# Second batch's attention: scores of pairs 2 to 4 in one piece each, ahead of the preceding pair's weighted sums, with a fourth buffer for exponentials

## The chip, the cores and the metric

The kernel runs on one core of one Trainium2 chip. The metric is the device time of one execution in microseconds (us); the kernel before took 550.68 us, the median of three runs. Five engines work side by side: TensorE (PE in the profile; PEld is its weight loading), VectorE (DVE), ScalarE (ACT), GpSimd (POOL) and SyncE, whose queue (SP) issues all DMA transfers of this kernel. Each executes its own instructions in order and waits on semaphores for the others.

## The reference

Attention for 4 batches x 8 heads, 768 positions, 64 features a head. A query sees the keys less than 16 positions away and, for each of 24 blocks of 32 positions, one block key (the elementwise maximum of the block) with one block value (the mean). The result, with the heads side by side (768 x 512 a batch), goes through a mixer of tokens and then of channels:

```python
k_sum = k.reshape(B, H, nb, block, D).max(axis=3)
v_sum = v.reshape(B, H, nb, block, D).mean(axis=3)
scores_all = np.concatenate([scores_l_m, scores_s], axis=-1)   # local (masked), blocks + log(block)
a = np.exp(scores_all - max); a = a / (sum(a) + 1e-09)
x = np.matmul(a, v_all)
h = np.maximum(xt @ w_tok1, 0.0) @ w_tok2
u = x + h.transpose(0, 2, 1)
h2 = np.maximum(u @ w_ch1, 0.0) @ w_ch2
return u + h2
```

All is float32; the kernel gets that accuracy on TensorE by splitting operands into a high and a low part and adding three products.

## The kernel before

**Attention.** Heads go in pairs: pair p holds heads n = 2p and 2p + 1, and batch b holds pairs 4b to 4b + 3. So batch 1, the "second batch" of the title, holds pairs 4 to 7. A pair's 12 query tiles of 64 rows are taken in two halves g of six. A query tile meets 96 local keys and 24 block keys, 120 columns. `scores` (L439) writes 24 matmuls a half, or 48 in one piece for both (tiles `sc_n_g`, one PSUM bank each); DVE subtracts and finds the lowest (`lowest`), ACT takes the exponentials (`power`) into the buffer `e_p_g`, with a sum in `den`. The exponentials are then turned: in batch 1 by TensorE (`turn_halves`, L521: `et_*` in PSUM, `eT_*` in SBUF), in batches 2 and 3 by DVE and a way through HBM (`turn_blocks`, L581: a transpose on DVE, a store `away_*`, and four fetches `eT_*`). `weighted` (L618) multiplies with the values (`av_n`, L637). `turn_x` and `fetch_x` send the result through HBM to have it turned: `xaway_b_half_p`, and back as `xT_b_half_p` in four fetches, issued in L608.

**Mixer.** `tok1x` (L818) makes token products: for each g three groups `t1q_b_g` of 12 matmuls on operand sets xs and ws, which ACT and POOL split, in a ring "u0" with four places (two sets). `split_t1` makes the two parts of `t1` from it (L784 on ACT, L789 on DVE). `tok2` (L872) multiplies with w_tok2 (`up_b_half_p`, L895); DVE adds it to `xT` (L912), ACT and DVE split the sum into `u`. Channel mixing runs over two halves of the tokens (512 and 256) and 12 blocks f of 128 channels: `ch1` (L947, `hp_b_half_f`, L956), a rectifying split into `h` on ACT and DVE, `ch2` (L983, `acc_b_half_o`, L999). At the end of a half DVE and POOL add `u` (L1030, L1038), and the result goes out (L1049).

**What sets the order.** Every operation is recorded by `add` with an estimated duration, what it reads and writes, and a rank; `Plan._order` schedules the list by these estimates, and every engine's instructions, the DMA issues on SP too, are written in that order and executed in it. The program records 24 slots of channel mixing for each batch (2 halves x 12 blocks f) and, at given slots, steps of the next batch's attention (`att_step`, L700: "s" scores, "e" turning, "a" weighted sums), token products (t1s), and up pieces (u1s, t2s). For batch 1 the steps follow `ORDER`, in halves, spread over the slots by a count (want); for batches 2 and 3 `PLACES` gives slots. Buffers are rings: "e" has 3 places for e, eT and xT; "h" 2; "u0" 4. PSUM banks rotate too: in the second half of a batch's slots the scores, the turnings, t1q and up share four banks (`att_bank`, `tok_bank`).

Of the kernel before, what the change touches and what calls it, by code (L numbers as in the profile page):

```python
# [15 lines left out]
AF = mybir.ActivationFunctionType  # L16
# [4 lines left out]
B, H, S, D = 4, 8, 768, 64  # L21
# [55 lines left out]
class Plan:  # L77
# [48 lines left out]
    def _order(self):  # L126
# [19 lines left out]
        while events:  # L146
# [5 lines left out]
            for e, queue in queues.items():  # L152
# [50 lines left out]
def tile_attention_mixer(  # L203
# [22 lines left out]
    def sbuf(shape, tag, name, bufs, dtype=F32):  # L226
        return plan.slot(sb, shape, dtype, tag, name, bufs)
# [211 lines left out]
    def scores(p, gs, behind=()):  # L439
# [3 lines left out]
        for g in gs:  # L443
            e = e_t[p, g] = sbuf([P, 2, HS], "e", f"e_{p}_{g}", 3)
# [243 lines left out]
    ORDER = [("s", 0, 0), ("s", 0, 1)]  # L688
    for hp in range(NP):
        more = hp + 1 < NP  # L690
        ORDER += [("e", hp, 0)] + [("s", hp + 1, 0)] * more
        ORDER += [("e", hp, 1), ("a", hp, 0)] + [("s", hp + 1, 1)] * more
    PAIR = [("s", None), ("e", 0), ("e", 1), ("a", 0)]
    STEPS = len(ORDER)
    FIRST = list(ORDER)
    for hp in range(NP - 1):
        at = FIRST.index(("a", hp, 0))
        FIRST[at : at + 2] = FIRST[at + 1], FIRST[at]

    def att_step(b, s, behind=()):  # L700

        if b >= FAR:
            hp, (kind, g) = s // 4, PAIR[s % 4]
        else:
            kind, hp, g = (ORDER if b else FIRST)[s]
# [936 lines left out]
    PLACES = {2: {}, 3: {}}  # L1642
    for b, ss, aa in ((2, (-1, 2, 6, 11), (0, 6, 11, 17)), (3, (-1, 2, 6, 11), (2, 6, 11, 14))):
        for hp in range(NP):
            PLACES[b].setdefault(ss[hp], []).extend(range(4 * hp, 4 * hp + 3))
            PLACES[b].setdefault(aa[hp], []).append(4 * hp + 3)
    start = [sum(HT[0][j // NF] // 256 for j in range(i)) for i in range(2 * NF + 1)]
    for b in range(B - 1):
        done = 0
# [16 lines left out]
        for slot, (half, f) in enumerate(seq):  # L1666
# [59 lines left out]
            if b == B - 3 and slot >= 2 * NF - 5:  # L1726
                weight_away(slot - 2 * NF + 5)
            if b == B - 2 and slot >= NF + 5:
                weight_away(slot - NF)
            if b == B - 2 and slot == 22:  # L1730
                last_sums()
            if slot == 2 * NF - 1 and b + 2 < B:
                for s in PLACES[b + 2].get(-1, ()):
                    att_step(b + 2, s, here)
# [64 lines left out]
```

## Time and profile before

| | us |
|---|---|
| runs of the kernel before | 550.59, 550.68, 554.17; median 550.68 |
| the profiled execution, its own time | 552.68 |
| its span in the profile | 550.2 |
| PE busy | 536.8 (98%) |
| DVE, POOL, ACT busy | 341.9, 268.1, 267.9 |

The profile shows one execution. Its span begins with the first and ends with the last instruction that the profiler recorded; the execution's own time is 2.5 us longer. A stretch of the span can be looked at alone, for busy time and for TensorE's granted clock. The chain of waits follows the work that ended last back through what released each step; its pieces have the length from their start to the start of the next piece, so a group of matmuls is a little shorter there than in the timeline, where matmuls are pipelined and ends are modelled.

### The profile page before, as it was taken

What the parts mean: (1) busy time and instruction counts of PE and PEld (TensorE: products, weight loads), DVE (VectorE), ACT (ScalarE), POOL (GpSimd) and SP (SyncE); (2) the same over time, 40 slices, a digit from 0 to 9 for tenths busy, and PEclk for the clock granted to TensorE, in tenths of its full rate; (3) what the DMA queues carried; (4) which work ended last, traced back from release to release, by engine and by line L of the source; (5) the groups of instructions that cost most, each with busy time, mean ns of one, the idle gap of its engine ahead of it and who ended that gap; (6) DMA issues with size and microseconds to landing.
All of it is one profiled execution on the core that took longest, in us unless ns stands there. A gap on an engine that the chain in (4) does not pass through costs nothing.

```text
span 550.2 us, 12919 instructions
## 1 busy us (share of the span) xinstructions
PE 536.8 (98%) x4649; PEld 479.6 (87%) x4649; DVE 341.9 (62%) x954; ACT 267.9 (49%) x771; POOL 268.1 (49%) x348
## 2 busy tenths in 40 slices
PE   7999999999999999989999999999999999999997
PEld 4789888878999987868899997888899999999997
DVE  4996779666656664535473363635264387687886
ACT  4897888755664331404062341414153354666652
POOL 2656688713037020488696321169888512445111
PEclk9999999999999999989999999999999999999999
DMA  8953788654657385867777756655858553643521
GB/s 324 397 201 116 220 270 238 222 171 146 210 178 222 63 239 106 231 172 233 214 261 184 189 194 152 207 120 174 198 160 219 149 222 125 195 141 118 189 97 57
DMA packets 148127, 103.46 MB, mean 188 GB/s; under 512 B 101216, under 2 KB 126048, under 8 KB 148064
## 3 DMA queue, kind: packets, MB, share of 16 engines
q1 hardware_dynamic: 147920, 102.55, 62.7%
q8 instruction: 36, 0.59, 0.4%
q14 instruction: 27, 0.22, 0.1%
q10 hardware_dynamic: 144, 0.10, 0.1%
HBM read 70.96 MB, written 29.88 MB: 183 GB/s over the span
## 4 chain that ended last, share of the span: by engine, by line
PE 85%; DMA 5%; DVE 5%; SPq 1%; POOL 1%; issue 1%; ACT 0%; DVEq 0%; ACTq 0%; POOLq 0%
PE hp L956 25%; PE acc L999 25%; PE up L895 5%; PE t1q L851 5%; PE av L637 4%; PE pb L1234 3%; PE qb L1234 3%; PE sc L468 3%; PE qc L1234 2%; PE pa L1234 2%; PE pc L1234 2%; PE qa L1234 2%; PE t1p L803 2%; DMA k<-in_kw 2%; DMA vw<-in_vw 2%; DVE t L1078 1%
## 5 line engine op out<-in xcount | busy, mean ns | idle before, releaser
L999 PE MATMUL acc<-h,w 128*128 128x512 f32 (+1 forms) x864 | 161.7, 336 | 0.7 <-DVE h L973 0.7
L956 PE MATMUL hp<-u,w 128*128 128x512 f32 (+1 forms) x864 | 160.8, 337 | 0.3 <-DVE h L973 0.3
L999 PEld LDWEIGHTS acc<-h,w 128*128 128x128 f32 x864 | 132.6, 188 | 19.4 <-issue 1.4
L956 PEld LDWEIGHTS hp<-u,w 128*128 128x128 f32 x864 | 133.5, 189 | 18.3 <-issue 0.8
L968 ACT ACTIVATE h<-hp 128x512 fp32r<-128x512 f32 (+1 forms) x72 | 35.3, 490 | 128.2 <-PE hp L956 120.0
L492 ACT ACTIVATE e<-e,den 128x120 f32<-128x120 f32 x192 | 69.9, 384 | 45.8 <-DVE den L482 43.7
L973 DVE SCALAR_TENSOR_TENSOR h<-hp,h 128x512 fp32r<-128x512 f32 (+1 forms) x72 | 39.9, 554 | 75.8 <-ACT h L968 75.4
L1076 POOL TENSOR_TENSOR s<-s,w 128x256 f32<-128x256 f32 x84 | 61.6, 739 | 5.2
L482 DVE CUSTOM_DVE_ANT_0 e<-sc,mask_sb 128x120 f32<-128x120 f32 x192 | 41.2, 277 | 14.4 <-PE sc L468 14.1
L1038 POOL TENSOR_TENSOR ot<-ot,u 128x512 f32<-128x512 f32 (+1 forms) x24 | 23.7, 1013 | 37.1 <-DVE ot L1030 16.4
L837 POOL TENSOR_TENSOR xs<-x,xs 128x512 fp32r<-128x512 f32 x18 | 23.3, 1294 | 35.1 <-ACT xs L832 35.0
L1605 POOL TENSOR_TENSOR w<-wb,w 128x256 fp32r<-128x256 f32 x48 | 34.5, 740 | 10.9 <-ACT w L1599 10.6
L895 PE MATMUL up<-wt,t 128*128 128x512 f32 (+2 forms) x192 | 38.0, 340 | 0.9 <-DVE den L482 0.9
L895 PEld LDWEIGHTS up<-wt,t 128*128 128x128 f32 x192 | 30.8, 189 | 3.8 <-PE sc L468 1.1
L420 DVE TENSOR_REDUCE vs<-vb 96x8 f32<-96x256 f32 (+1 forms) x40 | 18.2, 458 | 22.0 <-DMA vb<-in_vb 21.7
L637 PEld LDWEIGHTS av<-v,eT 120*64 120x64 f32 x768 | 24.7, 141 | 6.1 <-issue 5.0
L637 PE MATMUL av<-v,eT 120*64 120x64 f32 (+1 forms) x768 | 27.3, 228 | 2.2 <-DMA eT<-away 2.1
L851 PE MATMUL t1q<-xs,ws 128*128 128x256 f32 x216 | 28.5, 282 | 0.0
L492 ACT ACTIVATION_READ_ACCUMULATOR e<-e,den 128x1 f32 x144 | 27.2, 189 | 0.0
L851 PEld LDWEIGHTS t1q<-xs,ws 128*128 128x128 f32 x216 | 26.9, 190 | 0.1
L837 POOL TENSOR_TENSOR ws<-wt,ws 128x512 fp32r<-128x512 f32 x18 | 23.7, 1319 | 4.1 <-ACT ws L832 4.0
L468 PE MATMUL sc<-k,q 64*64 64x120 f32 x768 | 24.8, 268 | 0.9 <-DVE k L1078 0.8
(131 smaller groups left out, 833.5 us busy)
## 6 DMA issues: line engine op xcount, KB each, us to landing
w<-in_w_ch SPq DMA_DIRECT2D x48, 256.0 KB
k<-in_kw SPq DMA_DIRECT2D x16, 720.0 KB
v<-in_vw SPq DMA_DIRECT2D x24, 288.0 KB
q<-in_q SPq DMA_DIRECT2D x16, 384.0 KB
away<-e SPq DMA_DIRECT2D x16, 384.0 KB
eT<-away SPq DMA_DIRECT2D x64, 96.0 KB
sums<-s SPq DMA_DIRECT2D x24, 256.0 KB
w2d<-w SPq DMA_DIRECT2D x12, 512.0 KB
```

The source lines that it names most:

```text
L468: nc.tensor.matmul(tiles[g, j].t[c * QT : (c + 1) * QT, i * NC : (i + 1) * NC], lhsT=qt.t[rows, t * QT : (t + 1) * QT], rhs=kt.t[rows, t, ...
L482: nc.vector.tensor_tensor_reduce(out=e_t[p, g].t[:, j, i * P : i * P + NC], in0=tiles[g, j].t[:, i * NC : (i + 1) * NC], in1=mask_sb[:, mv ...
L492: nc.scalar.activation(ei, ei, AF.Exp, bias=den_t[n].t[:, 1, T : T + 1], scale=-1.0, accum_out=den_t[n].t[:, 0, T : T + 1] if p >= NP else ...
L637: nc.tensor.matmul(pv[cs, T], lhsT=eT(T % (TT // 2), c), rhs=v.t[:NC, 2 * T + c], start=True, stop=True,)
L837: lambda slot=slot, src=src: nc.gpsimd.tensor_tensor(out=slot.t[:, 1], in0=src(), in1=slot.t[:, 0].bitcast(F32), op=ALU.subtract),
L851: nc.tensor.matmul(pt.t[:, 2 * P * k : 2 * P * (k + 1)], lhsT=ws[:, wp, T, ks], rhs=xs[:, xp, T], start=(c == 0 and k == 0 and T == 0 and ...
L895: nc.tensor.matmul(pt.t[:, :nt], lhsT=t1.t[:, part, ks], rhs=wt2[w].t[:, k, h0 : h0 + nt], start=(far and k == 0 and i == 0), stop=(k == D ...
L956: nc.tensor.matmul(pt.t[:, :nt], lhsT=w1_t[f].t[:, w, c], rhs=us[c].t[:, part], start=(i == 0), stop=(i == len(ops) - 1),)
L973: lambda: nc.vector.scalar_tensor_tensor(out=h.t[:, 1], in0=pt.t[:, :nt], scalar=0.0, in1=h.t[:, 0].bitcast(F32), op0=ALU.max, op1=ALU.sub ...
L999: nc.tensor.matmul(slot.t[:, c0 : c0 + nt], lhsT=w2_t[f].t[:, w, o * P : (o + 1) * P], rhs=h.t[:, part], start=(f == 0 and w == 0 and part ...
L1076: nc.gpsimd.tensor_tensor(out=out_, in0=left, in1=right, op=op)
L1234: nc.tensor.matmul(bank_.t[:, cs], lhsT=w(i), rhs=x(j)[:, cs], start=first and n == 0, stop=True, skip_group_check=True,)
```

## The change

Scores of pairs 5 to 7 (2 to 4 of batch 1) are recorded as one piece of 48 matmuls instead of two of 24, ahead of the weighted sums of the preceding pair (`LAPPED`); since both halves of a pair's exponentials are then alive beside the turned ones of the preceding pair, the second half of each takes its place in the ring "h" instead of "e". The turnings of pairs 5 and 6 are one job on TensorE (both halves); those of pairs 4 and 7 stay in halves. The slots of batch 1's steps stand in a table, and slots of the steps around them move: weighted sums of batches 2 and 3, the token products of batch 1 (t1s of b = 0), up pieces of second halves (u1s), values loads of batch 3 and weight stores by a slot. The planner counts 0.4 us more for a DMA whose issue takes over 0.6 us. Batch 0's own steps keep their order under another notation (`FIRST`).

```diff
-                    w.end = dma + self.LAND
+                    w.end = dma + self.LAND + (0.4 if w.took > 0.6 else 0.0)
...
-            e = e_t[p, g] = sbuf([P, 2, HS], "e", f"e_{p}_{g}", 3)
+            tag, bufs = ("h", 2) if g and NP < p < 2 * NP else ("e", 3)
+            e = e_t[p, g] = sbuf([P, 2, HS], tag, f"e_{p}_{g}", bufs)
...
-    def turn_halves(p, g):
+    def turn_halves(p, gs):
...
         add(
-            "pe", 0.7, flip, reads=[(e, part) for part in PARTS],
-            writes=[(pt, 0) for pt in banks], rank=R_H,
+            "pe", 0.35 + 0.35 * len(gs), flip,
+            reads=[(e, part) for e, _, _ in parts for part in PARTS],
+            writes=[(pt, 0) for _, _, banks in parts for pt in banks], rank=R_H,
         )
...
+    HALVED = (0, 3)
+    PAIR = [("s", None), ("e", None), ("a", 0)]
+    def att_step(b, step, behind=(), halves=False):
...
+        elif kind == "e" and b < FAR:
+            for gs in [(0,), (1,)] if halves or hp in HALVED else [(0, 1)]:
+                turn_halves(p, gs)
...
+    LAPPED = [("s", 0, 0), ("s", 0, 1), ("e", 0, None)]
+    for hp in range(1, NP):
+        LAPPED += [("s", hp, None), ("a", hp - 1, 0), ("e", hp, None)]
+    LAPPED += [("a", NP - 1, 0)]
+    for step, at in zip(LAPPED, (9, 10, 11, 12, 13, 13, 13, 15, 15, 17, 17, 17, 18)):
+        PLACES[1][at].append(step)
+    for b, ss, aa in ((2, (-1, 2, 6, 11), (2, 6, 11, 19)), (3, (-1, 2, 6, 11), (2, 6, 9, 14))):
...
-            a0, a1 = 20, 30
-            t1s = (20, 22)
+            t1s = (17, 23)
...
-            u1s = ((2, 2, 3, 3), (0, 1, 2, 4))[b - 1]
+            u1s = ((1, 2, 3, 3), (0, 2, 3, 5))[b - 1]
...
-            if b == 1 and 1 < slot <= 17:
-                vb_step(3, slot - 2, here)
-            if b == 1 and 1 <= slot < 17:
-                vb_load(3, slot - 1)
+            if b == 1 and 2 < slot <= 18:
+                vb_step(3, slot - 3, here)
+            if b == 1 and 2 <= slot < 18:
+                vb_load(3, slot - 2)
...
-            if b == B - 3 and slot >= 2 * NF - 5:
-                weight_away(slot - 2 * NF + 5)
-            if b == B - 2 and slot >= NF + 5:
+            if b == B - 3 and slot >= 2 * NF - 4:
+                weight_away(slot - 2 * NF + 4)
+            if b == B - 2 and slot >= NF + 4:
```

What this does to the order on the engines is shown at three places. Lines of the changed kernel have numbers 2 higher; the last number in a name only tells buffers apart.

**1. TensorE, batch 1's attention, from the scores of pair 6 (`sc_12`, `sc_13`) on.** Of each group the first row is given. Before:

```order
L468 MATMUL sc_12_0_2099<-k_6_1775,q_6_1780 64x120
...
L956 MATMUL hp_0_1_3_2113<-u_0_1_0_1007,w1_3_1193 128x256 x3
...
L999 MATMUL acc_0_1_0_1994<-h_0_1_2_2064,w2_2_1145 128x256 x6
...
L637 MATMUL av_10_2158<-v_10_1954,eT_5_0_2084 64x64 x6
...
L468 MATMUL sc_12_1_2192<-k_6_1775,q_6_1780 64x120
...
L956 MATMUL hp_0_1_4_2211<-u_0_1_0_1007,w1_4_1236 128x256 x3
...
L535 MATMUL et_6_0_0_2231<-identf_66,e_6_0_2126 120x64
...
L999 MATMUL acc_0_1_0_1994<-h_0_1_3_2154,w2_3_1206 128x256 x6
...
L468 MATMUL sc_14_0_2274<-k_7_2018,q_7_2036 64x120
...
L956 MATMUL hp_0_1_5_2290<-u_0_1_0_1007,w1_5_1302 128x256 x3
...
L535 MATMUL et_6_1_0_2315<-identf_66,e_6_1_2225 120x64
```

After:

```order
L469 MATMUL sc_12_0_2180<-k_6_1775,q_6_1780 64x120
...
L469 MATMUL sc_12_1_2182<-k_6_1775,q_6_1780 64x120
...
L1001 MATMUL acc_0_1_0_1908<-h_0_1_4_2163,w2_4_1263 128x256 x6
...
L958 MATMUL hp_0_1_6_2237<-u_0_1_0_1007,w1_6_1371 128x256 x3
...
L641 MATMUL av_10_2261<-v_10_2048,eT_5_0_2143 64x64 x6
...
L1001 MATMUL acc_0_1_0_1908<-h_0_1_5_2208,w2_5_1318 128x256 x6
...
L958 MATMUL hp_0_1_7_2321<-u_0_1_0_1007,w1_7_1416 128x256 x3
...
L539 MATMUL et_6_0_0_2344<-identf_66,e_6_0_2226 120x64
...
L539 MATMUL et_6_1_0_2346<-identf_66,e_6_1_2251 120x64
...
L1001 MATMUL acc_0_1_0_1908<-h_0_1_6_2278,w2_6_1403 128x256 x6
...
L958 MATMUL hp_0_1_8_2395<-u_0_1_0_1007,w1_8_1481 128x256 x3
...
L469 MATMUL sc_14_0_2413<-k_7_1977,q_7_1983 64x120
```

The second half of the scores moved up to the first (24 + 24 matmuls, one piece), ahead of pair 5's weighted sums (`av_10`), and the two turnings `et_6_0` and `et_6_1` stand together. Each step stands three to four blocks f of batch 0's channel mixing later than before.

**2. TensorE and SP, the turn from batch 0 to batch 1.** On TensorE from the last token products (`t1q_1_1`) to the first channel mixing of batch 1 (`hp_1_0_0`), of each group the first row (of the scores the first and the last tile's). Before:

```order
L851 MATMUL t1q_1_1_2717<-xs_1_1_1_2713,ws_1_1_1_2731 128x256 x12
L851 MATMUL t1q_1_1_2717<-xs_1_1_2_2746,ws_1_1_2_2749 128x256 x12
L956 MATMUL hp_0_1_10_2796<-u_0_1_0_1007,w1_10_1605 128x256 x3
...
L999 MATMUL acc_0_1_0_1994<-h_0_1_9_2686,w2_9_1588 128x256 x6
...
L895 MATMUL up_1_0_2_2842<-wt2_0_810,t1_1_2_2812 128x512
...
L895 MATMUL up_1_0_3_2851<-wt2_0_810,t1_1_3_2814 128x512
...
L956 MATMUL hp_0_1_11_2861<-u_0_1_0_1007,w1_11_1662 128x256 x3
...
L999 MATMUL acc_0_1_0_1994<-h_0_1_10_2834,w2_10_1637 128x256 x6
...
L468 MATMUL sc_16_0_2899<-k_8_2528,q_8_2534 64x120
...
L468 MATMUL sc_17_1_2902<-k_8_2528,q_8_2534 64x120
...
L999 MATMUL acc_0_1_0_1994<-h_0_1_11_2893,w2_11_1692 128x256 x6
...
L956 MATMUL hp_1_0_0_2960<-u_1_0_0_2791,w1_0_929 128x512 x3
```

After:

```order
L1001 MATMUL acc_0_1_2_1909<-h_0_1_11_2677,w2_11_1692 128x256 x6
L853 MATMUL t1q_1_1_2808<-xs_1_1_0_2762,ws_1_1_0_2778 128x256 x12
L897 MATMUL up_1_0_0_2828<-wt2_0_810,t1_1_0_2796 128x512
...
L897 MATMUL up_1_0_1_2844<-wt2_0_810,t1_1_1_2798 128x512
...
L853 MATMUL t1q_1_1_2808<-xs_1_1_1_2803,ws_1_1_1_2821 128x256 x12
L853 MATMUL t1q_1_1_2808<-xs_1_1_2_2838,ws_1_1_2_2842 128x256 x12
L897 MATMUL up_1_0_2_2912<-wt2_0_810,t1_1_2_2901 128x512
...
L897 MATMUL up_1_0_3_2923<-wt2_0_810,t1_1_3_2905 128x512
...
L469 MATMUL sc_16_0_2941<-k_8_2408,q_8_2411 64x120
...
L469 MATMUL sc_17_1_2944<-k_8_2408,q_8_2411 64x120
...
L958 MATMUL hp_1_0_0_2972<-u_1_0_0_2891,w1_0_929 128x512 x3
...
L958 MATMUL hp_1_0_1_3009<-u_1_0_0_2891,w1_1_1030 128x512 x3
```

The last five groups of batch 0's channel mixing (hp 10 and 11, acc 9 to 11) stood among these pieces; they now stand ahead of them all, the last of them directly ahead of `t1q_1_1`. On SP, the fetches of `xT_1_0_*` and the writes of batch 0's second output half (`out_0<-ot_0_1_0`), before:

```order
L608 DMA xT_1_0_2_2752<-xaway_1_0_2_2466 32x16x32 x4
L291 DMA vb_2_11_2793<-in_vb 96x256
L608 DMA xT_1_0_3_2810<-xaway_1_0_3_2688 32x16x32 x4
L291 DMA vb_2_12_2849<-in_vb 96x256
L291 DMA vb_2_13_2876<-in_vb 96x256
L608 DMA xT_1_1_0_2927<-xaway_1_1_0_2013 32x8x32 x2
L291 DMA vb_2_14_2937<-in_vb 96x256
L291 DMA k_10_2941<-in_kw 128x1440
...
L1049 DMA out_0<-ot_0_1_0_2957 128x256
L608 DMA xT_1_1_1_2987<-xaway_1_1_1_2246 32x8x32
L1049 DMA out_0<-ot_0_1_0_2957 128x256 x2
```

After:

```order
L612 DMA xT_1_0_2_2785<-xaway_1_0_2_2595 32x16x32 x2
L291 DMA vb_2_13_2801<-in_vb 96x256
L612 DMA xT_1_0_2_2785<-xaway_1_0_2_2595 32x16x32 x2
L1051 DMA out_0<-ot_0_1_0_2780 128x256
L612 DMA xT_1_1_0_2835<-xaway_1_1_0_2092 32x8x32 x2
L291 DMA vb_2_14_2852<-in_vb 96x256
...
L612 DMA xT_1_1_1_2871<-xaway_1_1_1_2342 32x8x32 x2
L291 DMA vb_2_15_2888<-in_vb 96x256
L1051 DMA out_0<-ot_0_1_0_2780 128x256
L612 DMA xT_1_1_1_2871<-xaway_1_1_1_2342 32x8x32
L1051 DMA out_0<-ot_0_1_0_2780 128x256
L612 DMA xT_1_0_3_2903<-xaway_1_0_3_2760 32x16x32 x4
```

The four fetches of `xT_1_0_3` stood ahead of every such write; they now stand behind three of them, and behind the fetches of `xT_1_1_0` and most of `xT_1_1_1`. On POOL the first of the output additions stands behind the split of ws for the fourth of the six t1q groups, and the others behind the last ws.

**3. DVE, pair 9 (the second of batch 2), from the first transpose of its exponentials on.** Before:

```order
L589 STREAM_TRANSPOSE e_9_0_3215<-e_9_0_3215 128x768
L420 TENSOR_REDUCE vs_3_3159<-vb_3_2_3255 96x8
...
L589 STREAM_TRANSPOSE e_9_1_3219<-e_9_1_3219 128x768
...
L912 TENSOR_TENSOR xT_1_1_2_3139<-up_1_1_2_3314,xT_1_1_2_3139 128x256
...
L351 TENSOR_REDUCE ks_11_3349<-k_11_3259 128x24
L1078 SCALAR_TENSOR_TENSOR k_11_3259<-ks_11_3349 128x12x24
```

After:

```order
L593 STREAM_TRANSPOSE e_9_0_3199<-e_9_0_3199 128x768
L914 TENSOR_TENSOR xT_1_1_2_3094<-up_1_1_2_3278,xT_1_1_2_3094 128x256
L914 TENSOR_TENSOR xT_1_1_3_3143<-up_1_1_3_3288,xT_1_1_3_3143 128x256
L420 TENSOR_REDUCE vs_3_3206<-vb_3_1_3240 96x8
...
L351 TENSOR_REDUCE ks_11_3327<-k_11_3256 128x24
L593 STREAM_TRANSPOSE e_9_1_3203<-e_9_1_3203 128x768
...
L1080 SCALAR_TENSOR_TENSOR k_11_3256<-ks_11_3327 128x12x24
```

The block keys' maximum for pair 11 (`ks_11`, which reads the load of `k_11`) stood behind the second transpose and now stands ahead of it. On SP a load of values (`vb_3_3`) stood ahead of the second store of the exponentials and now stands between the two lots of four fetches.

## Rows read from the trace of the kernel before

**Rows 1.** The page's first lines: span, and busy time of each engine with its share of the span and its instructions.

```profile
span 550.2 us, 12919 instructions
...
PE 536.8 (98%) x4649; PEld 479.6 (87%) x4649; DVE 341.9 (62%) x954; ACT 267.9 (49%) x771; POOL 268.1 (49%) x348
```

**Rows 2.** Stretches of the span. Columns: stretch, its length and PE busy (instructions), then PEld, DVE, ACT and POOL the same way, then the granted clock of TensorE (1.00 is full speed), DMA share, GB/s.

```profile
40.00:210.00 170.00, 170.00 (x1423) 148.09 (x1422) 113.47 (x314) 105.77 (x314) 79.12 (x105) 1.00 0.64 188
...
230.00:240.00 10.00, 8.09 (x72) 6.67 (x71) 2.50 (x6) 0.60 (x1) 7.93 (x13) 0.88 0.65 127
```

**Rows 3.** What TensorE waited for over the whole span: waiting group, what released it, us in total, times, longest.

```profile
PE av L637 <- DMA eT<-away: 2.1, 2, 1.9
...
PE up L895 <- DVE den L482: 0.9, 1, 0.9
...
PE acc L999 <- DVE h L973: 0.7, 1, 0.7
PE hp L956 <- DVE h L973: 0.3, 1, 0.3
```

**Rows 4.** The chain of waits from 104 to 150 us, the attention of batch 1 among the channel mixing of batch 0. Columns: start, length up to the next piece of the chain, what. The matmuls L956 and L999 have 512 columns up to 129 us and 256 after it.

```profile
120.24 0.49 PE et L535 x12
...
131.07 1.61 PE hp L956 x12
132.68 0.78 PE sc L468 x24
...
135.03 1.36 PE hp L956 x12
136.39 0.84 PE et L535 x24
...
142.65 1.55 PE av L637 x48
```

**Rows 5.** The same view further on, where the scores of a pair of batch 2 stand in one piece.

```profile
245.78 1.39 PE sc L468 x48
247.17 2.94 PE acc L999 x12
```

**Rows 6.** The timeline of PE at the end of batch 0 (start, length, line, operation, out<-in, count).

```profile
165.05 1.58 PE L851 MATMUL t1q<-xs,ws 128*128 128x256 f32 x12
...
177.99 3.04 PE L851 MATMUL t1q<-xs,ws 128*128 128x256 f32 x24
180.86 1.54 PE L956 MATMUL hp<-u,w 128*128 128x256 f32 x12
...
183.60 2.90 PE L895 MATMUL up<-wt,t 128*128 128x512 f32 x12
...
189.25 1.46 PE L468 MATMUL sc<-k,q 64*64 64x120 f32 x48
```

**Rows 7.** The timelines of ACT, POOL and DVE over the same stretch (one after the other); in brackets the idle time before and what ended it.

```profile
166.72 0.63 ACT L832 ACTIVATE xs<-x 128x512 fp32r<-128x512 f32 x1 [2.17 <-PE t1q L851]
...
181.06 0.66 ACT L784 ACTIVATE t<-t1q 128x256 fp32r<-128x256 f32 x2 [0.76 <-PE t1q L851]
...
168.67 1.51 POOL L837 TENSOR_TENSOR ws<-wt,ws 128x512 fp32r<-128x512 f32 x1
...
192.15 2.82 POOL L1038 TENSOR_TENSOR ot<-ot,u 128x256 f32<-128x256 f32 x4 [4.65 <-DVE ot L1030]
...
181.75 0.76 DVE L789 SCALAR_TENSOR_TENSOR t<-t1q,t 128x256 fp32r<-128x256 f32 x2
```

**Rows 8.** The timeline of the SP queue (first two rows) and of DVE (last row): issues of the turned attention result's way back, and the first addition that waited for such a transfer.

```profile
181.05 2.59 SPq L608 DMA_DIRECT2D xT<-xaway  x4
...
314.05 1.40 SPq L608 DMA_DIRECT2D xT<-xaway  x2
...
317.57 0.69 DVE L912 TENSOR_TENSOR xT<-up,xT 128x512 f32<-128x512 f32 x1 [0.40 <-DMA xT<-xaway]
```

**Rows 9.** The timeline of PE around pair 9's scores.

```profile
217.25 1.46 PE L468 MATMUL sc<-k,q 64*64 64x120 f32 x48
219.56 0.95 PE L895 MATMUL up<-wt,t 128*128 128x256 f32 x6 [0.85 <-DVE den L482]
...
234.81 0.57 PE L637 MATMUL av<-v,eT 120*64 120x64 f32 x12
```

**Rows 10.** The chain of waits from 221 to 243 us, from the turning of pair 9's exponentials to the matmuls after its weighted sums.

```profile
222.48 6.95 DMA away<-e
...
234.36 2.79 DMA eT<-away
...
237.29 1.98 PE av L637 x36
239.27 3.79 PE hp L956 x12
```

**Rows 11.** Stretches of 2 us around that wait, columns as in the stretches above.

```profile
238.00:240.00 2.00, 2.00 (x26) 1.79 (x24) 1.21 (x3) 0.00 (x0) 0.81 (x3) 0.50 0.61 188
240.00:242.00 2.00, 2.00 (x8) 1.57 (x8) 1.18 (x2) 0.00 (x0) 1.84 (x4) 0.75 0.87 207
```

**Rows 12.** The timeline of DVE behind the turning of pair 9, and of SP behind its fetches.

```profile
227.51 0.95 DVE L351 TENSOR_REDUCE ks<-k 128x24 f32<-128x768 f32 x1 [0.30 <-DMA k<-in_kw]
...
235.12 0.59 SPq L291 DMA_DIRECT2D vb<-in_vb  x1
```

More of the change, by code (lines that the diff above doesn't have):

```diff
@@ new lines, in turn_halves @@
+    def turn_halves(p, gs):
+        parts = []
+        for g in gs:
+            pair = sbuf([P, 2, 2, HS // 2], "e", f"eT_{p}_{g}", 3)
+            banks = [att_bank(f"et_{p}_{g}_{c}", True) for c in range(2)]
+            parts += [(e_t[p, g], pair, banks)]
+            for j in range(2):
+                eT_t[2 * p + j, g] = (
+                    lambda i, c, j=j, pair=pair: pair.t[:NC, c, j, i * QT : (i + 1) * QT]
+                ), [(pair, c) for c in range(2)]
+        def flip():
+            for e, _, banks in parts:
+                for j, i in PARTS:
+                    for c, pt in enumerate(banks):
+                        rows, at = slice(QT * c, QT * (c + 1)), (TT // 2 * j + i) * QT
+                        nc.tensor.matmul(
+                            pt.t[:NC, at : at + QT], lhsT=e.t[rows, j, i * P : i * P + NC],
+                            rhs=identf[rows, rows], start=True, stop=True, is_transpose=True,
+                        )
+        add(
+            "pe", 0.35 + 0.35 * len(gs), flip,
+            reads=[(e, part) for e, _, _ in parts for part in PARTS],
+            writes=[(pt, 0) for _, _, banks in parts for pt in banks], rank=R_H,
+        )
+        for _, pair, banks in parts:
+            for c, pt in enumerate(banks):
+                add(
+                    "act", 0.49,
+                    lambda c=c, pt=pt, pair=pair: nc.scalar.activation(
+                        pair.t[:NC, c].rearrange("p j k -> p (j k)"), pt.t[:NC, :HS], AF.Copy
+                    ),
+                    reads=[(pt, 0)], writes=[(pair, c)], rank=R_EVAC,
+                )
@@ L684, in weighted @@
             )
-    ORDER = [("s", 0, 0), ("s", 0, 1)]
+    FIRST = [("s", 0, 0), ("s", 0, 1)]
     for hp in range(NP):
         more = hp + 1 < NP
[L691 to L705, printed above, removed]
-        p = b * NP + hp
-        if kind == "e":
-            (turn_blocks if b >= FAR else turn)(p, g)
+        FIRST += [("e", hp, 0)] + [("s", hp + 1, 0)] * more + [("e", hp, 1)]
+        FIRST += [("s", hp + 1, 1)] * more + [("a", hp, 0)]
+    HALVED = (0, 3)
+    PAIR = [("s", None), ("e", None), ("a", 0)]
+    def att_step(b, step, behind=(), halves=False):
+        kind, hp, g = step
+        p = b * NP + hp
+        if kind == "e" and b == 0:
+            turn(p, g)
+        elif kind == "e" and b < FAR:
+            for gs in [(0,), (1,)] if halves or hp in HALVED else [(0, 1)]:
+                turn_halves(p, gs)
+        elif kind == "e":
+            for g in range(2):
+                turn_blocks(p, g)
         elif kind == "a":
@@ L1628, in tile_attention_mixer @@
     key_blocks(0)
-    for s in range(STEPS):
-        att_step(0, s)
+    for step in FIRST:
+        att_step(0, step)
     for tick in range(6, 10):
@@ L1732, in tile_attention_mixer @@
             if slot == 2 * NF - 1 and b + 2 < B:
[L1733 to L1734 removed]
+                for step in PLACES[b + 2][-1]:
+                    att_step(b + 2, step, here)
             ch2(b, half, f)
```

43 lines of the change are left out of this document (5 added, 38 removed).

## The prediction

> **What bounds the kernel now.** The page comes first: TensorE (PE) is busy 536.8 of 550.2 us, the next engine 341.9 [rows 1]. The stretches show where the other 13 us lie: from 40 to 210 us PE is busy without a gap, at the full granted clock [rows 2], so the attention of batch 1, which the change rearranges, makes no wait there to be removed. Past the start and the tail, the table of waits gives all that is left: 2.1 + 0.9 + 0.7 + 0.3 = 4.0 us [rows 3]. Nearly half is one wait, 1.91 us for the exponentials of pair 9 to come back from HBM, and it costs more than itself: the 36 matmuls behind it took 1.98 us where 48 at full speed take 1.55 (so 36 take 1.16), and the next group 3.79 us where 2.94 is usual after narrow matmuls [rows 4, 5, 10]. That is 0.82 + 0.85 = 1.67 us. The stretches of 2 us say why: the granted clock is 0.50 there (the 1.2 GHz level), then 0.75, behind the wait of 1.91 us [rows 2, 11].
>
> So the change can gain in two ways only: fewer or cheaper pieces on PE, or a part of these 4 (with the clock 5.7) us. It can lose wherever PE, now gapless, gets a wait.
>
> **A. Fewer pieces in batch 1.** The change removes no matmul. It joins three pairs of score halves. A half takes 0.78 us on the chain [rows 4], a whole 1.39 [rows 5]: 2 x 0.78 - 1.39 = 0.17 each, 0.5 for three. One turning of exponentials that stood in two pieces (pair 6; pair 5's already stood together) becomes one: 2 x 0.49 - 0.84 = 0.14 [rows 4]. A wide group right after narrow matmuls takes 1.61 us instead of 1.36 [rows 4], 0.25 each time; the order drops about two such returns: 0.5. Sum -1.1; bounds 0 (if a busy PE gives nothing back) and -1.5 (two returns more). I take -1.1, since the pitches are of this very code.
>
> The Trainium skill ("Perfetto Trace Analysis", Identifying the Most-Contended Engine) says that matmul busy time misjudges TensorE, because matmuls are pipelined, and that weight-load busy time is the measure. By the busy column this part could give 0; by that rule the stretch with PEld at 148.09 of 170 still has room in it. The pitches side with the rule.
>
> The fourth buffer and the planner's 0.4 us cost nothing by themselves; they act through the order.
>
> **B. The turn from batch 0 to batch 1.** The order uses up its channel mixing earlier: before, hp 10, acc 9, hp 11, acc 10 and acc 11 stood between the last t1q, the up pieces, the scores of pair 8 and the first hp of batch 1. After, t1q, up, scores and hp stand bare. Those five groups are still executed, ahead, so they cost nothing more; what they covered now shows. Three places:
>
> B1. The operand sets of t1q (xs, ws) have two places, and the next may be made only when the t1q before last has read its own. Before, that t1q ended at 165.05 + 1.58 = 166.63, ACT began at 166.72 and POOL ended at 168.67 + 1.51 = 170.18 [rows 6, 7]: 3.55 us. After, PE has between the second and the fourth t1q only half an acc (0.7), a t1q (2.87 / 2 = 1.44, from 177.99 to 180.86 [rows 6]) and half an acc: 2.8. New wait 0.75; bounds 0 (POOL's second in 1.3 instead of 1.51 and ACT prompt) and 1.5 (an output addition, 2.82 / 4 = 0.71 [rows 7], slips between on POOL).
>
> B2. Behind the last t1q stands up piece 2, which needs t1's high part from ACT and its low part from DVE: 0.66 and 0.76 us for two [rows 7]. One half of each is 0.33 and 0.38; the third matmul needs the low part. 0.05 + 0.33 + 0.38 less two matmuls (2 x 0.23, of 12 in 183.60 to 186.34 [rows 6]) is a wait of about 0.45; bounds 0 and 1.1 (both halves first on each engine).
>
> B3. The dearest. Scores of pair 8 use four PSUM banks that the up pieces leave; the second half needs the one of piece 3, free when DVE has added it to xT_1_0_3. Those four fetches stood on SP ahead of all writes of the output; now they stand behind three of them, and the third waits for POOL's third output addition, which stands behind the last ws. From the start of the last t1q (POOL has just ended that ws): two additions 1.42 [rows 7], a semaphore 0.1, the write's issue 0.4, four fetches 2.6 [rows 8], landing 2.1 (issues ended 315.45, the addition began 317.57 [rows 8]) to 2.8 [rows 10], the addition 0.7: 7.3 to 8.0. PE needs 1.44 + 0.45 + 2.74 + 0.70 (half of 1.39) = 5.3 to the same point, with B2's wait. New wait 2.0; bounds 0 (the last t1q starts late, after POOL has gone on) and 6 (landing as slow as 6.95 [rows 10]). I take 1.8, near the lower end, because a fetch of the same kind has 2.1.
>
> B in sum +3.0. Two groups queue behind B3's wait on PE: the first hp, whose inputs need the same addition, and all after it.
>
> **C.** The wait of 0.85 us of an up piece for a den (DVE's scores ahead of it in the queue) [rows 3, 9] goes: an acc group (2.7 us) now stands between the scores of pair 9 and that piece. -1.0 with the halting first two matmuls; bounds 0 and -1.0.
>
> **D. The wait of 1.91 us.** From the scores' start at 217.25 to the last turned block's landing at 234.36 + 2.79 = 237.15 is 19.9 us; PE comes there after 17.56 + 0.46 = 18.0 [rows 9, 10]. After, PE has the acc more (2.75) and the wait of C less (0.85): 19.9. With the chain as before, the wait would be gone. But the chain gets longer: the second transpose now stands behind ks_11, which waits for k_11 (227.51) and takes 0.95 [rows 12]; its store goes out about 229.45 instead of 226, SP's fetches behind it start 0.4 later, and a vb load (0.59 [rows 12]) stands between the two lots of fetches: 0.9 to 1.0 more. Wait 1.0 instead of 1.9, -0.9, the clock falling as before. Bounds: -3.6 (1.91 + 1.67, wait and low clock gone) and +3 (the second store lands after 6.95 us like the first [rows 10], and the wait is 5).
>
> **E.** The 0.3 and 0.7 us [rows 3] lie in stages whose placements move by a slot or two; I take half, -0.5, bounds 0 and -1.0. The vb loads and weight stores of later slots are SP work with PE busy beside it: 0.
>
> **Sum.** -1.1 + 3.0 - 1.0 - 0.9 - 0.5 = -0.5. The profiled execution took 552.68 us by its own time, 2.5 more than its span; it would become 552.2. The median of the runs is 550.68, so the forecast is 550.2.
>
> **Rivals.**
> 1. *As above: the turn gives back what the pieces save.* 547.7 to 552.7, chance 0.50.
> 2. *The transfers and splits at the turn are hidden, and pair 9's data comes in time.* For it: additions on DVE and POOL idle before the rows of [rows 7]; PE's 19.9 equals the chain's. Against: the SP and DVE orders. With B at 1.0 and D at -3.6: -1.1 + 1.0 - 1.0 - 3.6 - 0.5 = -5.2, 545.5; with D alone 547.5. Range 545.2 to 547.7, chance 0.28.
> 3. *Slower: xT_1_0_3 lands late and TensorE's clock falls at the turn.* The price is B3 at 4 instead of 1.8 (+2.2) and the 1.67 of the low clock, 550.2 + 3.9 = 554.1; with the clock alone 551.9. For it: the 1.91 us wait was followed by clock 0.50 [rows 11]; against: the 0.85 one was not (PE works at the usual pace behind it). It decides from a wait of about 1.9 us at the second half of pair 8's scores. Chance 0.15. The Trainium skill ("TensorE: Matmul & The Clock Gate", HAM oscillation) says that waits for transfers can put TensorE back to half rate each time; by that rule alone this rival would be the likeliest. The trace shows it once, at [rows 11].
> 4. *It doesn't do what it says.* PE is busy throughout, so joined pieces free nothing: A is 0, 551.3. The pitches of [rows 4, 5] speak against. Chance 0.07.
>
> **Numbers.** A median of this kernel can be told from no change at about 1%, 5.5 us. Range 545.5 to 553.5: it holds rival 1 and 4, nearly all of 2, and part of 3. Faster than 545.2 needs rival 2 whole and more: 0.13. Slower than 556.2 needs rival 3 with D's upper bound: 0.05. The rest, 0.82, is within 1%. The likeliest case's own range is 547.7 to 552.7.
>
> **What would show it.** In the profile after: three L469 groups x48 of some 1.4 us before 165 us (A). At the turn, waits of PE for ACT or POOL at t1q (B1), for DVE's t at up (B2), and for an addition of xT, released by a DMA, at the scores of pair 8 (B3). No wait of up for den (C). The wait of av for eT, shorter, and the granted clock beside it (D). The prediction is wrong if batch 0 doesn't hand over about 1 us earlier in PE's work, if the turn waits under 1 or over 5 us, or if the clock at pair 9 stays full.

## The result, and the profile after

The changed kernel is slower: 555.07 us, median of 14 runs, against 551.51 of the kernel before (14 runs on the same chips); the ratio is 1.0064, with a 95% interval from 1.0044 to 1.0084, some 3.5 us. The time lies above the stated range (545.5 to 553.5). The profiled execution took 554.03 us, with a span of 552.2 against 550.2 [rows 1].

What TensorE waited for after the change (columns as in [rows 3]):

```profile
PE sc L469 <- DVE xT L914: 3.3, 1, 3.3
...
PE up L897 <- DVE t L791: 0.9, 1, 0.9
...
PE up L897 <- ACT t L786: 0.5, 1, 0.5
PE t1q L853 <- POOL ws L839: 0.4, 1, 0.4
PE hp L958 <- DVE h L975: 0.3, 1, 0.3
PE pb L1236 <- DVE s L1080: 0.2, 1, 0.2
```

All that [rows 3] showed is gone, but for the 0.3 of hp: no wait of av for eT, none of up for den, none of acc. In their place stand the three of the turn that the prediction named B1 to B3, the last nearly twice its size. The timeline of PE at the turn:

```profile
178.37 1.58 PE L853 MATMUL t1q<-xs,ws 128*128 128x256 f32 x12
...
181.23 1.46 PE L853 MATMUL t1q<-xs,ws 128*128 128x256 f32 x10 [0.35 <-POOL ws L839]
...
185.28 3.09 PE L853 MATMUL t1q<-xs,ws 128*128 128x256 f32 x24
188.84 0.73 PE L897 MATMUL up<-wt,t 128*128 128x512 f32 x2 [0.47 <-ACT t L786]
190.49 2.56 PE L897 MATMUL up<-wt,t 128*128 128x512 f32 x10 [0.91 <-DVE t L791]
192.98 1.03 PE L469 MATMUL sc<-k,q 64*64 64x120 f32 x26
197.32 0.84 PE L469 MATMUL sc<-k,q 64*64 64x120 f32 x22 [3.31 <-DVE xT L914]
198.09 7.33 PE L958 MATMUL hp<-u,w 128*128 128x512 f32 x24
```

The last row costs too: 24 hp matmuls at full speed take 5.6 us, here 7.33. The stretches (columns as in [rows 2]) have the granted clock under 1 there, down to 0.50 (the 1.2 GHz level) from 200 to 202 us, behind the wait, and at 1.00 where pair 9's wait was:

```profile
180.00:190.00 10.00, 8.75 (x56) 7.40 (x54) 5.81 (x11) 4.64 (x10) 8.95 (x9) 1.00 0.51 114
190.00:200.00 10.00, 6.20 (x64) 4.76 (x65) 5.25 (x21) 2.27 (x7) 0.57 (x3) 0.94 0.50 118
200.00:210.00 10.00, 10.00 (x43) 8.26 (x43) 6.38 (x23) 5.25 (x23) 0.90 (x1) 0.89 0.59 196
...
230.00:240.00 10.00, 10.00 (x46) 8.29 (x45) 5.44 (x10) 1.80 (x3) 7.94 (x11) 1.00 0.59 130
```

```profile
200.00:202.00 2.00, 2.00 (x6) 1.52 (x6) 1.65 (x13) 1.75 (x10) 0.00 (x0) 0.50 0.96 380
```

The timeline of SP shows why the fetch of xT_1_0_3 (the x4 at 191.20) went out so late, and that of DVE (first the two splits together, then the first of them alone, then the addition) what it took to arrive:

```profile
184.29 1.21 SPq L612 DMA_DIRECT2D xT<-xaway  x2
185.61 0.54 SPq L291 DMA_DIRECT2D vb<-in_vb  x1
186.20 2.53 SPq L612 DMA_DIRECT2D xT<-xaway  x4
188.84 0.53 SPq L291 DMA_DIRECT2D vb<-in_vb  x1
189.47 0.37 SPq L1051 DMA_DIRECT2D out<-ot  x1
189.90 0.56 SPq L612 DMA_DIRECT2D xT<-xaway  x1
190.51 0.59 SPq L1051 DMA_DIRECT2D out<-ot  x1
191.20 2.60 SPq L612 DMA_DIRECT2D xT<-xaway  x4
```

```profile
188.02 2.08 DVE L1080 SCALAR_TENSOR_TENSOR u<-xT,u 128x512 fp32r<-128x512 f32 x2
...
188.02 1.48 DVE L1080 SCALAR_TENSOR_TENSOR u<-xT,u 128x512 fp32r<-128x512 f32 x1
...
196.57 0.69 DVE L914 TENSOR_TENSOR xT<-up,xT 128x512 f32<-128x512 f32 x1 [2.73 <-DMA xT<-xaway]
```

SP issues without a gap. The buffer of xT_1_0_3 came free with the first of the two splits (u_1_0_0), which ran from 188.02 to 189.50; the fetch was issued 1.7 us later, behind the queue, and landed 3.33 us after the start of its last issue (the chain's row "DMA xT<-xaway"). In the kernel before the same fetch took 2.55 us, from 183.01 to 185.56.

The end of that landing is one straggler. A transfer reports its landing in 16 parts; 15 of the last one's came between 195.23 and 195.44, the sixteenth at 196.49. In runs 1 and 3 below it is the same: 15 parts by 193.42 and 194.59, the sixteenth at 195.75 and 195.96. In all three a transfer of 16 KB of instructions had ended 1.1 to 1.2 us before the sixteenth part (at 195.37, 194.55 and 194.86). That this transfer held the part up is likely, but not shown: no run moved it.

**Why the runs show more than the two profiles.** The profile of before has the low clock behind pair 9's wait [rows 11]; its runs seldom do. Over the 104 runs of before that stand beside the experiments, the mean granted clock was 0.997 or less in 23 (median 553.2 us) and 0.998 or more in 81 (median 550.7). After the change it was 0.993 to 0.997 in 14 of 14. So the change exchanged an occasional low clock for a constant one, and the profile read for the prediction was one of the occasional cases.

### The profile page after: what moved, and what is told of

The parts are those of the page before. It is cut to its first block, busy times and chain, and to the rows that moved or that the text cites. A ratio compares the mean times of both kernels' runs of the same rounds, so it can differ in the third digit from the quotient of the medians.

```text
span 552.2 us, 12942 instructions
## 1 busy us (share of the span) xinstructions
PE 536.4 (97%) x4649; PEld 479.3 (87%) x4649; DVE 342.2 (62%) x954; ACT 267.8 (48%) x771; POOL 269.0 (49%) x348
## 4 chain that ended last, share of the span: by engine, by line
PE 88%; DMA 4%; DVE 3%; ACT 1%; POOL 1%; SPq 1%; issue 1%; DVEq 0%; ACTq 0%; POOLq 0%
PE hp L958 27%; PE acc L1001 27%; PE up L897 5%; PE t1q L853 4%; PE av L641 4%; PE qb L1236 3%; PE pb L1236 3%; PE sc L469 3%; PE qc L1236 2%; PE qa L1236 2%; PE pc L1236 2%; DMA k<-in_kw 2%; PE pa L1236 2%; PE t1p L805 2%; DMA q<-in_q 1%; DVE e L483 1%
## 5 line engine op out<-in xcount | busy, mean ns | idle before, releaser
L469 PEld LDWEIGHTS sc<-k,q 64*64 64x64 f32 x768 | 19.9, 133 | 9.9 <-DVE xT L914 3.5
L1078 POOL TENSOR_TENSOR u<-xT,u 128x256 fp32r<-128x256 f32 x8 | 6.0, 759 | 45.1 <-ACT u L924 39.8
```

What stands on the lines that cost most here:

```text
L469: nc.tensor.matmul(tiles[g, j].t[c * QT : (c + 1) * QT, i * NC : (i + 1) * NC], lhsT=qt.t[rows, t * QT : (t + 1) * QT], rhs=kt.t[rows, t, ...
L1078: nc.gpsimd.tensor_tensor(out=out_, in0=left, in1=right, op=op)
```

## The experiments

Each kernel was compared with the kernel before on the same chip; "clock low in n of m" counts runs with a mean granted clock of 0.997 or less. "Cover" is other work on TensorE that stands between a group and its inputs' arrival. In the diffs, "..." marks what is left out.

**1. Only batch 1's part.** The slots of batches 2 and 3 and the planner's number go back:

```diff
-                    w.end = dma + self.LAND + (0.4 if w.took > 0.6 else 0.0)
+                    w.end = dma + self.LAND
...
-            u1s = ((1, 2, 3, 3), (0, 2, 3, 5))[b - 1]
+            u1s = ((2, 2, 3, 3), (0, 1, 2, 4))[b - 1]
...
```

> The changed kernel with only its batch-1 part (joined scores, fourth buffer, merged turnings, table of slots, token products at 17 and 23); the planner's 0.4 us and all slots of the steps for batches 2 and 3 as before. Theory A (the loss is made at the turn from batch 0 to batch 1, where up, scores and hp stand bare): the waits there stay, 4 to 5.5 us with a granted clock under 1 behind them, and the time is that of the changed kernel or a little less, 552 to 556. Rival B (the loss comes from the moved slots of batches 2 and 3 or from the planner's number): at or under the kernel before, 548 to 551.

554.76 us, ratio 1.0070 [1.0042, 1.0097], clock low in 9 of 12. The scores wait 4.2 us for xT. The loss is made by batch 1's part; B is out. The fetch of xT_1_0_3 went out at 188.98 here, 2.2 us sooner than in the changed kernel, and landed only 0.7 us sooner (195.75 instead of 196.49), 4.80 us after the start of its last issue: the queue alone does not set the time.

**2. Only the rest.** The kernel before with the moved slots and the planner's number.

> The complement: the kernel before with the planner's 0.4 us and all the moved slots for batches 2 and 3, but batch 1's attention in halves and in its old order. Theory A: the turn keeps its cover (no wait over 0.5 us there), while pair 9's wait of 1.9 us with its low clock and the waits of up and acc go, as in the changed kernel: 4 to 5 us under the kernel before, 545.5 to 548. Rival B: 552 to 555. If pair 9's wait needs batch 1's part to go, it stays and the time is 549 to 551.

551.84 us, ratio 1.0010 [0.9988, 1.0031]: no gain, which Theory A had expected. The turn has no wait, but two others came, and part of pair 9's stayed:

```profile
PE av L637 <- issue: 1.7, 1, 1.7
PE acc L999 <- DVE h L973: 1.7, 1, 1.7
...
PE av L637 <- DMA eT<-away: 0.8, 1, 0.8
```

The first is at pair 8's weighted sums (212.5 us). So the moved slots by themselves are worth nothing here, and the waits of pairs 8 and 9 were not seen in the changed kernel together with a kept cover at the turn.

**3. Block-value loads of batch 2 four slots earlier**, TensorE's order untouched:

```diff
-            if b == 0 and 11 <= slot < 19:
+            if b == 0 and 7 <= slot < 15:
...
-                    vb_load(2, 2 * (slot - 11) + c)
+                    vb_load(2, 2 * (slot - 7) + c)
```

> The changed kernel with batch 2's block-value loads and sums recorded four slots earlier; TensorE's order stays the same, instruction for instruction. They leave the SP queue and DVE's queue at the turn. Theory A1 (the wait for xT_1_0_3 was longer than forecast because SP and DVE stood behind those loads): the wait of the scores falls from 3.3 to 1.5 to 2.2 us, that of up for t from 0.9 to under 0.3, the clock stays up, and the time is 2 to 4 us under the changed kernel, 550.5 to 552.5. Rival A2 (the fetch can't start earlier, since its buffer comes free with the split that the last token products release, and its landing is slow): the wait stays over 2.7 us and the time within 1 us of the changed kernel.

554.94 us, ratio 1.0067 [1.0040, 1.0093], clock low in 6 of 6; the scores still wait 3.4 us for xT. The wait of up for DVE's part of t went, the fetch started at 190.22 instead of 191.20, and it landed 3.76 us after the start of its last issue. A1 falls as far as those loads go: fetches and writes that stay in SP's queue filled the room.

**4. Work in the wait.** 14 unread matmuls between the two halves of pair 8's scores:

```diff
...
+                for _ in range(FILL if idle and g else 0):
+                    nc.tensor.matmul(
+                        idle.t[:, :512], lhsT=wt2[0].t[:, 0, :P], rhs=wt2[0].t[:, 0, :512],
+                        start=True, stop=True,
+                    )
```

> The changed kernel with 14 matmuls of 512 columns, whose result nobody reads, written on TensorE between the two halves of pair 8's scores, 3.2 us of work where it waited 3.3 us; everything else keeps its order. If the wait brings the granted clock down: the clock stays 1.00 from 190 to 210 us, the 24 hp matmuls behind take 5.6 instead of 7.3 us, and the time is 1.7 us under the changed kernel, about 552.5 to 553.5. If something else lowers the clock (the shorter waits ahead, the narrow matmuls): the 24 stay at 7 us and the time is that of the changed kernel or up to 1 us more.

552.94 us, ratio 1.0029 [1.0011, 1.0048], clock low in 0 of 12. Two rows of PE and a stretch over both:

```profile
192.60 3.47 PE L469 MATMUL idle<-wt 128*128 128x512 f32 x14
...
197.04 5.73 PE L968 MATMUL hp<-u,w 128*128 128x512 f32 x24
```

```profile
190.00:200.00 10.00, 10.00 (x84) 7.64 (x83) 5.52 (x28) 3.30 (x13) 0.43 (x2) 1.00 0.54 125
```

The waiting time is as long, and the clock stays up: the wait itself brought it down. Against the changed kernel (1.0064) that is 0.35%, nearly 2 us, close to the 7.33 - 5.73 = 1.6 of the rows; the two intervals overlap a little, so the rows and the clock of the twelve runs carry this more than the ratios.

**5. Another place for xT_1_0_3**, the ring x, whose place is free after the first three t1q:

```diff
         tag, bufs = (("e", 3), ("ot", 2))[half]
+        if (b, half, p) == (1, 0, 3):
+            tag, bufs = "x", 2
```

> The changed kernel with xT_1_0_3 (the buffer whose fetch the scores of pair 8 waited for) in the ring x, in the place that batch 1's first two pairs' attention result leaves after the first three token products, instead of the ring e, where it had to wait until u_1_0_0 was split. TensorE's and DVE's orders stay the same; on SP its four fetches move ahead of the writes of the output. Theory A2 (that buffer starts the chain): the wait of 3.3 us falls under 1 us, the granted clock stays 1.00 behind it, and the turn gives back 4 to 5 us; the time is 549.5 to 551, unless TensorE, now earlier, meets a new wait at the weighted sums of pair 8 (20.8 us after its scores began the exponentials weren't back in the second experiment): then 551 to 553. If the fetch is late for another reason, the wait stays over 2 us and the time at 554 to 555.

550.78 us, ratio 0.9988 [0.9969, 1.0008], clock low in 0 of 12. One row of the waits:

```profile
PE sc L469 <- DVE xT L916: 0.5, 1, 0.5
```

3.3 became 0.5, and the whole loss is gone; no new wait at pair 8. A2 holds in this: the late fetch, and the clock that fell with it, was the loss. The edit also takes the fetch out from behind the writes on SP (its last issue ended at 186.10), and it lands ahead of the load of instructions (193.53), so it doesn't tell the parts of the ring, the queue and the straggler apart; by the rows of the changed kernel the ring would have allowed 189.5, and the queue made it 191.2.

**6. Both edits (3 and 5).**

> Both single edits together: xT_1_0_3 in the ring x, and batch 2's block-value loads and sums four slots earlier; TensorE's order as in the changed kernel. If the block-value loads matter once the buffer does not bind: the wait of up for t falls from 0.9 to under 0.5 and the time is 0.5 to 1 us under that of the buffer alone. If not, the two are equal within 0.5 us.

550.29 us, ratio 0.9983 [0.9961, 1.0005]: equal to run 5 within its interval. The wait of up for DVE's part of t is gone, but t1q waits 0.7 and an acc 0.6.

**7. Cover held back.** Batch 0's last hp may not start before the last t1q (`t1q_w`, new, keeps the recorded token products):

```diff
...
+                if (b, slot) == (0, 23):
+                    at.behind.add(t1q_w[1, 1, 2])
```

> The changed kernel with batch 0's last hp held back on TensorE until the last token products are through (so hp 11 stands between them and up, and acc 11 between up and the scores of pair 8); nothing else is edited. If the loss is missing cover at the end of the turn: the waits of up (1.4 us) go, that of the scores falls from 3.3 to 1 us or less with the clock staying up, and the time is 3 to 5 us under the changed kernel, 549.5 to 551.5. If cover can only be moved (the token products ahead, whose operand sets take 3.5 us to make again, lose it): new waits of 3 to 4 us for POOL's ws appear and the time is within 1.5 us of the changed kernel.

551.11 us, ratio 0.9992 [0.9971, 1.0014], clock low in 1 of 12. Its waits at and after the turn:

```profile
PE av L641 <- DMA eT<-away: 1.4, 1, 1.4
...
PE t1q L855 <- POOL ws L841: 0.8, 1, 0.8
...
PE t1q L855 <- POOL xs L841: 0.5, 1, 0.5
PE hp L960 <- DVE xT L916: 0.4, 1, 0.4
```

The waits of up and scores are gone. t1q lost 1.3 us for it, not the 3 to 4 of the second theory: 1.4 us of hp and 1.4 of acc cover more behind the last t1q than ahead of it.

**8. The kernel before with its own wait filled**, 16 unread matmuls at pair 9:

```diff
+                    for _ in range(16 if n == 18 and T == TT // 2 else 0):
+                        nc.tensor.matmul(
+                            pt.t[:, 384:], lhsT=wt2[0].t[:, 0, :P], rhs=wt2[0].t[:, 0, :P],
+                            start=True, stop=True,
+                        )
```

> The kernel before with 16 matmuls of 128 columns, whose result nobody reads, written on TensorE at the place of pair 9's wait of 1.9 us, about 1.9 us of work; the order of everything else is that of before. If that wait brings the clock down there: the clock stays 1.00 from 236 to 242 us, the hp behind takes 2.9 instead of 3.8 us, and the time is 1.2 to 1.7 us under the kernel before (549 to 549.5). If the clock falls for another reason: no difference or up to 0.5 us more.

551.75 us, ratio 1.0000 [0.9980, 1.0021], clock low in 1 of 12. In its profile the clock is up (the hp behind takes 3.06 us instead of 3.86) and the span is 548.7, but the time does not move, where 549 to 549.5 was expected: most runs of before (29 of 35 here) have no low clock to give back.

**9. Scores recorded in halves again**, all else as changed:

```diff
-        LAPPED += [("s", hp, None), ("a", hp - 1, 0), ("e", hp, None)]
+        LAPPED += [("s", hp, 0), ("s", hp, 1), ("a", hp - 1, 0), ("e", hp, None)]
...
-    for step, at in zip(LAPPED, (9, 10, 11, 12, 13, 13, 13, 15, 15, 17, 17, 17, 18)):
+    for step, at in zip(LAPPED, (9, 10, 11, 12, 12, 13, 13, 13, 13, 15, 15, 17, 17, 17, 17, 18)):
```

> The changed kernel with the scores of pairs 5 to 7 recorded in halves again (the fourth buffer, the merged turnings, the token products' slots and all else stay). A half needs two PSUM banks instead of four, so pair 5's first half starts in the first half of batch 0's mixing, as before the change, and the attention of batch 1 ends earlier; pairs 6 and 7 still have their two halves side by side. If the late end of the attention is what laid the turn bare: hp 10, hp 11 and acc groups stand among the token products and up again, the waits there are under 1 us in all, the clock stays up at 190 to 210 us, and the time is that of the kernel before or 1 to 2 us less, 549 to 551. If the loss is of another kind: 553 to 555.

549.69 us, ratio 0.9975 [0.9954, 0.9997], clock low in 2 of 12. The end of the turn in PE's timeline:

```profile
180.94 1.60 PE L853 MATMUL t1q<-xs,ws 128*128 128x256 f32 x12
182.38 1.54 PE L958 MATMUL hp<-u,w 128*128 128x256 f32 x12
183.76 1.52 PE L1001 MATMUL acc<-h,w 128*128 128x256 f32 x12
185.12 2.90 PE L897 MATMUL up<-wt,t 128*128 128x512 f32 x12
187.85 1.58 PE L1001 MATMUL acc<-h,w 128*128 128x256 f32 x12
189.36 1.46 PE L469 MATMUL sc<-k,q 64*64 64x120 f32 x48
```

Cover is back, with no wait in these rows. The scores of pairs 6 and 7 still run as 48 together: the planner puts the halves side by side. Pair 5 starts at 126.06 us instead of 131.95, and the last weighted sums at 168.05 instead of 171.44.

**10. Halves, with both edits of 6.**

> The halves of the run before with the two edits that freed the turn's transfers (xT_1_0_3 in the ring x, block-value loads four slots earlier). If what is left after the buffer's edit is the bare t1q and up (1.7 to 2.2 us of waits): it is 1 to 2 us under the kernel before, 548.5 to 550, and the fastest of all. If the waits only move on to pair 8's or 9's weighted sums, as in the second experiment: within 0.5 us of the kernel before.

548.14 us, ratio 0.9936 [0.9911, 0.9961], clock low in 0 of 12: faster than both kernels. The only profile is of the slowest of the twelve runs (551.69 us); its waits are 1.0 us of the scores for xT, 1.0 of pair 9's weighted sums and 1.8 of weighted sums in batch 1 (146.7 us). So a wait at pair 9 did come, as the second case had it, and the time came as in the first; what a typical run gains where is not shown.

**11. Cover held back, with both edits of 6.**

> Batch 0's last hp held back behind the last token products, with the same two edits. The waits of t1q for POOL (1.3 us when hp was held back alone) and of pair 8's weighted sums (1.4 us) should stay, that of hp for xT (0.4 us) go: 0.3 to 0.6 us under that run, 550 to 551. If it is 1 us or more under it, the late xT also held up pair 8.

549.38 us, ratio 0.9962 [0.9941, 0.9983]. The wait of pair 8's sums fell from 1.4 to 0.5, so the late transfers had held up pair 8 as well; which of the two edits freed it is not separated.

**12. Only pair 5 in halves.**

```diff
+    LAPPED += [("s", 1, 0), ("a", 0, 0), ("s", 1, 1), ("e", 1, None)]
-    for hp in range(1, NP):
+    for hp in range(2, NP):
...
-    for step, at in zip(LAPPED, (9, 10, 11, 12, 13, 13, 13, 15, 15, 17, 17, 17, 18)):
+    for step, at in zip(LAPPED, (9, 10, 11, 11, 12, 12, 13, 13, 15, 15, 17, 17, 17, 18)):
```

> The changed kernel with the scores of pair 5 alone in halves (the first in the first half of batch 0's mixing, as before the change); pairs 6 and 7 stay in one piece. The planner starts pair 5 earlier, but still writes hp 11 and the last acc ahead of the last token products, so the turn stays bare. If the bare turn is the cause, an earlier start alone does not help: the wait of the scores for xT stays over 2 us with a lower clock behind it, and the time is 553 to 555. If the late start of pair 5 is the cause by itself: 549 to 551, as with all three pairs in halves.

558.42 us, ratio 1.0124 [1.0084, 1.0163], clock low in 6 of 6, the slowest of all: scores wait 1.8 us, up 2.0, t1q 1.4, and later an acc 2.4. Pair 5 started at 125.97 us, as early as in 9. An early start alone is not what helps; the groups that stand between t1q, up and scores are. The time lies above both expected ranges, and part of it lies outside the turn: the acc wait of 2.36 us at 235.85 is followed by a granted clock of 0.50, and ten acc take 4.14 us there instead of 2.56. At the turn the clock fell earlier than in the changed kernel, behind the wait of up:

```profile
191.54 4.11 PE L897 MATMUL up<-wt,t 128*128 128x512 f32 x10 [1.46 <-DVE t L791]
```

against 2.56 us for the same ten there, behind a wait of 0.91. In run 2 the clock stayed at 1.00 behind waits of 1.7 us.

## Why the prediction was wrong, point by point

**The order was read rightly.** TensorE makes the turn bare, the three waits are B1 to B3, each with the releaser that was named, and runs 1, 9 and 12 tie the loss to it. Of the forecast's own signs of being wrong, two came: the turn waited 5.0 us (0.35 + 0.47 + 0.91 + 3.31, a little over 5), and the clock at pair 9 stayed full.

**B3 is the step that failed, by its size and by what stands ahead of the fetch.** It put the fetch's issue 1.9 us after the last t1q's start (186.8). It was issued at 191.20, 4.4 after. POOL was done in time (188.94). SP was not: from 184.29 on it had eleven other issues to make, of about 0.6 us each, which the order showed and the sum left out. And the buffer came free only at 189.50, with a split on DVE that the sum left out too. From the end of the last issue (193.80) to the addition (196.57) it took 2.8 us, where 2.1 was taken. Wait 3.31, where the terms gave 2.0 and, without a term for it, 1.8 was taken. B2 was 0.47 + 0.91 = 1.38 instead of 0.45 (its terms add up to 0.30): DVE subtracted both u splits (2.08 us from 188.02) before t's low part, the first in 1.48 us where the later ones take 0.69; why it was slow is open. B1 was 0.35, not 0.75.

The waits are not all that a halt costs: a group cut in two loses more than its idle time. Counted by starts, against the pitch (start to next start) of the same groups in [rows 5, 6], the four halts cost 0.6 (t1q, 180.49 to 182.53 instead of 1.44), 0.7 (t1q to up, 185.28 to 188.84 instead of 2.87), 1.4 (up, 188.84 to 192.98 instead of 2.74) and 3.7 (scores, 192.98 to 198.09 instead of 1.39): 6.4 us, where the waits add up to 5.0 and the forecast for B was 3.0.

**The clock is the step that was misplaced.** The sum let it fall at pair 9 before and after, for nothing. It fell at the turn (7.33 - 5.6 = 1.7 us; run 4 shows that it was the wait), and pair 9 had neither wait nor low clock. That was rival 3, "lands late and the clock falls at the turn", and 3.31 lies past its point of 1.9 us (run 12 shows that a wait of 1.46 us can be followed by it too). It had a chance of 0.15, and 554.1 as its time. The Trainium skill ("TensorE: Matmul & The Clock Gate", HAM oscillation) says that waits for transfers put TensorE back to half rate; the row of 200 to 202 us, at 0.50 behind a wait of 3.31 us, agrees, and so does run 4 from the other side.

**C, D and E.** C came as forecast. D went further: pair 9's wait went whole. TensorE reached those sums 19.4 us after the scores (222.21 to 241.60; forecast 19.9) and did not wait, so the chain had not grown to the 20.9 us that the forecast gave it; the first fetch was issued 11.1 us after the scores' start (233.29), and not later than the 12.2 of before (229.48). But its -1.67 for the clock, the lower bound, can't be counted against the median, since 81 of 104 runs of before had no such loss. E gave 0.7 - 0.2 = 0.5, as taken, which is luck: the 0.7 went whole, the 0.3 stayed, and a new 0.2 came.

**A.** Three wholes have the forecast pitch (131.95 to 133.34 is 1.39), and one more turning of 24 (0.84) stands in the profile: -0.6 of the -1.1. The whole of it shows between the first hp of batch 0 and the first of batch 1, before and after:

```profile
56.30 2.92 PE L956 MATMUL hp<-u,w 128*128 128x512 f32 x12
...
192.13 5.62 PE L956 MATMUL hp<-u,w 128*128 128x512 f32 x24
```

```profile
57.01 2.92 PE L958 MATMUL hp<-u,w 128*128 128x512 f32 x12
```

Before, that is 135.83 us without a wait; after, it is 141.08 (to 198.09), and less the 6.4 of the halts 134.7: 1.1 to 1.2 less, as A had it. Run 5's profile gives the same. How exact that is, runs 2 and 8 tell, which keep the order of before there: 135.83 and 136.38 us.

**The sum again**, with measured sizes: -0.5 as forecast, +3.4 (B, 6.4 instead of 3.0), -1.0 (D, pair 9's wait), +1.7 (clock): +3.6, where the runs show 3.5 us, from 2.4 to 4.6. The sizes come from one execution of each kernel, so the agreement is better than they can promise.

**What the change gives apart from it.** With the transfer freed (run 5) it is equal to the kernel before; with halves recorded and the loads earlier as well (run 10) it is 0.64% faster. By runs 9 and 12, recording the scores of pairs 6 and 7 whole was the harmful part: recorded as halves they come together anyway, and the turn keeps its cover.

## What to carry to other kernels

When work is moved ahead, ask what it covered: the groups were only executed earlier, and what they had hidden showed at the turn. For a transfer that becomes bare, count every issue ahead of it in its queue, and what frees its buffer, not only the last one that it waits for by name. And look at the granted clock over many runs before a loss of it is counted as the kernel's.

## What the runs showed of the hardware

Filling a wait with unread matmuls gave back nearly 2 us (run 4), though the wait's time was spent all the same. From the start of its last issue until its landing, the four-fetch transfer of xT_1_0_3 took 2.55 us (before), 3.33 (changed), 3.76 (run 3) and 4.80 (run 1, the chain's row); in the last three 1.05, 1.37 and 2.33 us of that were the wait for one part of sixteen. And the first 40 us, with the same 790 matmuls ahead of the first channel mixing in all these kernels, held from 33.24 (changed) to 35.37 us (run 12) of busy PE: profiles differ by 2 us there without an edit to that work, so spans of single executions don't rank kernels this close.
